# A second GEMM in two passes, with eight pairs of row blocks in the seven-product scheme

## The chip, the core and the metric

The kernel runs on one core of a Trainium2 chip. Its time is the device time of one execution in microseconds. The engines have short names throughout: PE (matmuls) with PEld (its weight loads), DVE (vector), ACT (scalar), POOL (GpSimd, which here only issues the accumulating transfers) and SP (which issues all other transfers).

## What is computed

The output is the sum of three terms over a sequence of S = 2048 rows with D = 1024 channels: the input itself, a gated long convolution, and a feed-forward network with F = 3584 hidden columns.

```python
xn = layernorm(q)                                   # rows of 1024
kv = short_causal_conv(k, shift_k, 4 taps) * v
y  = irfft(rfft(kv, 2S) * rfft(ssm_k, 2S))[:S] + kv * ssm_D
out = q + xn * y + silu(xn @ w1) @ w2               # w1: 1024 x 3584, w2: 3584 x 1024
```

Everything is f32. A matmul operand is split into two f16 parts, `hi` and `lo`, and a product takes three matmuls: hi.hi, hi.lo and lo.hi. The split is one ACT instruction (`hi`) and then one on DVE (`lo`), which needs ACT's result; `split` (L365) issues both.

## The kernel before

**Order of the work.** The kernel is a set of Python generators, each a stream of operations (`Op`) with an engine, an estimated duration, and what it reads and writes. `Order.run` (L165) keeps a clock of estimates and picks the stream whose next operation could start first, less a bias that is given to `add`. So the order on each engine is fixed when the program is built; on the chip each engine goes through its list in order and waits on semaphores. `L` issues a transfer on SP, `G` an accumulating one on POOL (the transfer engines add to what stands at the destination, in device memory or on chip), `T` a group of matmuls on PE. `Token` and `flag` tell a generator when it may go on. Buffers come from `Ring` (whole tiles) and `Halves` (tiles that are given out whole, `pair`, or by halves, `tile`): `wo` (six, operands of PE), `hfs` (three, f32 results), `hts` (two, split results on their way out), and eight `places` of one tile each, which hold the left operand blocks in the first GEMM and w2 in the second.

**First GEMM** (`units`, L1001, matmuls at L964 to L966): h = silu(xn @ w1). Rows go in two halves `sp`, columns in 14 pairs `i` of two blocks of 128. A pair of row blocks and a pair of column blocks make a 2 x 2 block product, done with seven products (`PRODUCTS`, L39) in place of eight; pairs 0 and 1 of the first half are done plainly. `evacuate` (L927) copies and sums the products, applies silu, and leaves four blocks: `up` and `low`, two each. Blocks of plain pairs are split and written to `hs` in device memory (`blocks`, L888). Blocks of the pairs in `PAIRS` (8, 9, 12, 13) go through `quad` (L845), which forms the seven left operands of the second GEMM (A11, A12, A22 and the sums S1 to S4), splits them, and writes them to `hsf`.

**Second GEMM** (`feed_forward`, L1050; matmuls at L1096 to L1098). A step is three matmuls of 128 x 128 weights and 512 columns. First the plain blocks: for each half `h` of the output columns and each of 16 row tiles, five chunks of four blocks, whose w2 lies in the places of `W2PLACE`; `result` (L1232) scales the sum and adds it to the output with `G`. Then `units2` (L1114): eight units of two row tiles by both column halves, seven products of four steps each. `evacuate2` (L1176) copies the shared partial sums between PSUM banks, sums two of the four results on DVE, and issues one transfer for each of four output tiles. `load_h` (L1240) loads the left operands in the order of use.

**w2** (`norms_w2`, L1283; `load_w2`, L1358). The raw rows come by SP into `wraw` or `hfs`; differences such as B22 - B12 are formed on DVE, with one place (`hold`) for sums that live on; `split` writes the factors into the places of `FPLACE`.

**Convolution** (`convolution`, L1394), in eight groups of 128 channels, interleaved with both GEMMs. For each group: `loads` and `load_v` fetch k, v and the filter; `gate` forms kv and its norms; `signal_parts` and `parts_of` split kv and the filter and transpose kv by a transfer; `stage1` multiplies by the DFT matrix; `transforms` runs an FFT of eight, the product of spectra and the inverse on DVE (`spec`, `tmp`); `result_parts`, `stage1_inv` and `gated` come back and add to the output (`yt`). The next group's `stage1` may write `spec` only where the last group has been read (`taken`). `copies` (L1256) puts x into the output before anything is added to it.

Of the kernel before, what the change touches and what calls it, by code (L numbers as in the profile page):

```python
# [20 lines left out]
P = 128  # L21
# [21 lines left out]
PAIRS = (8, 9, 12, 13)  # L43
# [3 lines left out]
W2PLACE = [(2, 7, 6, 3, 4), (0, 1, 5, 2, 7)]  # L47
FPLACE = (6, 3, 4, 0, 1, 5, 2, 7)
# [3 lines left out]
RAWS = {"B11": [(0, 0)], "B21": [(1, 0)], "B22": [(1, 1)], "T1": [(0, 1), (0, 0)], "T2": [(0, 0)],  # L52
        "T3": [(1, 1), (0, 1)], "T4": [(1, 0)]}
# [238 lines left out]
def h3_ffn_kernel(ctx, tc, x, kp, vs, fs, shift, dskip, w1, w2, cfwd, cinv, out):  # L292
# [82 lines left out]
    hs = [dram.tile([4, P, NF, 2, P], F16, name=f"hs{b}") for b in range(4)]  # L375
    ws = {i: {n: dram.tile([P, 2, KH, len(n) * P], F16, name=f"ws{i}_{n[0]}") for n in FACTORS} for i in range(2, NP)}
    xsp = {p[0]: dram.tile([P, 4, KH, 2, P], F16, name=f"xsp{p[0]}") for p in PRODUCTS.values()}
# [510 lines left out]
    def blocks(i, b, hf, tok, ready):  # L888
# [8 lines left out]
        for j in range(2):  # L897
            yield L(hs[b][:, :, 2 * i + j].rearrange("q p h s -> p q (h s)"),
                    ht[:, 4 * j:4 * j + 4].rearrange("p q h s -> p q (h s)"))
            ttok.set()  # L900
# [26 lines left out]
    def evacuate(i, b, one, c, made, seen):  # L927
# [5 lines left out]
        yield vs_r.ready  # L933
        u, ut = vs_r.tile([P, 4, P])
        yield made["P6"]
        yield a_act(u, two, AF.Copy)
# [4 lines left out]
        yield ws_r.ready  # L941
        d, dt = ws_r.tile([P, 4, P])
        yield made["P5"]
        yield a_act(d, two, AF.Copy)
        seen["P5"].set()
        low, done = yield from places_of(i, b + 1)
        yield v_tt(low[:, 1], c[0], d, ADD)
        dt.set()
# [4 lines left out]
        yield v_tt(low[:, 0], c[0], u, ADD)  # L953
        ut.set()
# [95 lines left out]
    def feed_forward():  # L1050
# [13 lines left out]
        for h in range(2):  # L1064
            for ts in TOGETHER[h]:
# [18 lines left out]
        flag["last part"].set()  # L1084
        yield from units2()


    TOGETHER = ([range(3)] + [(t,) for t in range(3, NT)],
                [(t,) for t in range(NT - 3)] + [range(NT - 3, NT)])

    def steps2(po, hx, wc, first, last, more=False, of=range(4), q=slice(0, W)):
        o = po[:, q]
        for n in of:
            def mm(n=n):
                kw = dict(skip_group_check=more)
                nc.tensor.matmul(o, hx[:, n, 0, :], wc[:, n, 0, q], start=first and n == 0, stop=False, **kw)  # L1096
                nc.tensor.matmul(o, hx[:, n, 0, :], wc[:, n, 1, q], start=False, stop=False, **kw)  # L1097
                nc.tensor.matmul(o, hx[:, n, 1, :], wc[:, n, 0, q], start=False, stop=last and n == 3, **kw)  # L1098
# [4 lines left out]
    def uses2():  # L1103

        yield 0, "P1"
        for u in range(len(tiles2)):
            for n in ("P7", "P6", "P2", "P5"):
                yield u, n
            if u + 1 < len(tiles2):
                yield u + 1, "P1"  # L1110
            yield u, "P3"
            yield u, "P4"

    def units2():  # L1114

        def product2(n, u, o, first=False, of=range(4), q=slice(0, W)):
            yield flag["h2", u, n]
            hx, htok = flag["h2", u, n].what
            yield flag["w2f", n]
            wc, wtok = w2f[n]  # L1120
            yield from steps2(o, hx, wc, first, True, not first, of, q)
            if 3 not in of or q.stop < W:
                return
            htok.set()
            if u == len(tiles2) - 1:
                wtok.set()

        yield ff.ready
        one = ff.tile([P, W])
        yield from product2("P1", 0, one[0], True)  # L1130
        for u in range(len(tiles2)):
            made, seen = defaultdict(Token), defaultdict(Token)
            last = u == len(tiles2) - 1
            yield ff.ready
            c = ff.tile([P, W])
            add(evacuate2(u, one, c, made, seen), EB)
            yield from product2("P7", u, c[0], True)
            yield seen["P1"]
            two = seen["bank"][0]
            yield from product2("P6", u, two)  # L1140
            made["P6"].set()
            if last:
                yield from product2("P2", u, one[0], of=(0, 1))
            else:
                yield from product2("P2", u, one[0])
                made["P2"].set()
            yield seen["P6"]
            yield from product2("P5", u, two)
            made["P5"].set()
            if last:  # L1150
                yield from product2("P2", u, one[0], of=(2, 3))
                made["P2"].set()
            else:
                yield ff.ready
                one = ff.tile([P, W])
                yield from product2("P1", u + 1, one[0], True)
            yield seen["P5"]
            yield from product2("P3", u, two)
            made["P3"].set()
            yield seen["P7"]  # L1160
            for q in columns(u):
                yield from product2("P4", u, c[0], q=q)
                made["P4", q.start].set()

    def columns(u):

        m = 2 if u == len(tiles2) - 1 else 1
        return [slice(a * W // m, (a + 1) * W // m) for a in range(m)]
# [7 lines left out]
    def evacuate2(u, one, c, made, seen):  # L1176
# [715 lines left out]
```

## Time and profile before

| | |
|---|---|
| median of 3 runs | 1251.4 us (1251.26 to 1251.9) |
| the profiled execution | 1250.78 us, span 1249.0 us |
| busy PE / PEld | 1227.0 us (98%) / 591.7 us (47%) |
| busy DVE / ACT / POOL | 1127.2 us (90%) / 749.5 us (60%) / 132.9 us (11%) |
| first GEMM's last matmuls, second's first | near 597 us |
| transfers | 292.9 MB: 266.9 MB by SP's queue (67.4% of the 16 transfer engines' span), 24.9 MB by POOL's (14.9%) |

A group's row reads: line, engine, operation, output<-inputs by the program's names, partitions x elements, xcount, then busy us and mean ns of one, then the idle time of the engine just before them and what ended it. Busy time of PE overstates its work, since matmuls overlap: their distance is what counts. L344, L347 and L355 are helpers that issue all sums, scaled sums and ACT instructions, so there the names of the tiles tell which step it is.

### The profile page before, as it was taken

The numbers are of one execution on the slowest core, as the hardware profiler recorded it, in microseconds if no ns is written. First come the engines' busy times: TensorE is split into PE (matmuls) and PEld (weight loads), VectorE is DVE, ScalarE is ACT, GpSimd is POOL, SyncE is SP. The second block draws the span as 40 slices with busy tenths as digits, with TensorE's granted clock in tenths as the row PEclk, the third lists the DMA queues.
The fourth block names the chain that finished last, engine by engine and source line by source line (L and its number), as shares of the span: only waits on it lengthen the run. The fifth ranks groups of instructions, "written<-read, shape, count | busy, mean of one in ns | idle before, by whom it ended". The sixth has DMA issues, their size and how long they took to land.

```text
span 1249.0 us, 17052 instructions
## 1 busy us (share of the span) xinstructions
PE 1227.0 (98%) x6017; PEld 591.7 (47%) x6017; DVE 1127.2 (90%) x1390; ACT 749.5 (60%) x1309; POOL 132.9 (11%) x141
## 2 busy tenths in 40 slices
PE   7899999999999999999999999999999999999998
PEld 6444544444444454445444544544454454445444
DVE  7999997889799979999899799889979979998992
ACT  6868897878767786757762632563273264526231
POOL 0000000000000030001110300310030030113114
PEclk8999999999999999999999999999999999999999
DMA  9358999889999898978998897689586587978766
GB/s 336 94 176 289 314 309 309 276 277 349 321 332 299 263 260 272 258 239 230 345 329 213 178 266 176 149 245 276 127 199 184 131 169 245 250 157 143 161 144 93
DMA packets 254293, 292.93 MB, mean 235 GB/s; under 512 B 48768, under 2 KB 167808, under 8 KB 252032
## 3 DMA queue, kind: packets, MB, share of 16 engines
q1 hardware_dynamic: 227472, 266.93, 67.4%
q0 software_dynamic: 26736, 24.92, 14.9%
q8 instruction: 47, 0.77, 0.2%
q14 instruction: 38, 0.31, 0.1%
HBM read 193.22 MB, written 98.57 MB: 234 GB/s over the span
## 4 chain that ended last, share of the span: by engine, by line
PE 69%; DVE 20%; issue 4%; DMA 4%; ACT 2%; POOL 0%; SPq 0%; DVEq 0%; POOLq 0%; ACTq 0%
PE ff L1096 10%; PE ff L1098 10%; PE ff L1097 10%; PE ff L966 10%; PE ff L964 10%; PE ff L965 10%; DVE spec L344 7%; DVE tmp L344 3%; DVE x L347 2%; PE ps L1563 2%; PE ps L1565 2%; PE ps L1564 2%; DVE spec L347 1%; DVE ht L347 1%; DMA out<-yt 1%
## 5 line engine op out<-in xcount | busy, mean ns | idle before, releaser
L1096 PE MATMUL ff<-x,wo 128*128 128x512 f16 x868 | 328.1, 378 | 1.0 <-DVE hf L347 0.6
L1098 PE MATMUL ff<-x,wo 128*128 128x512 f16 x868 | 328.1, 378 | 0.0
L1097 PE MATMUL ff<-x,wo 128*128 128x512 f16 x868 | 328.1, 378 | 0.0
L965 PE MATMUL ff<-x,wo 128*128 128x512 f16 (+1 forms) x808 | 303.9, 376 | 2.7 <-DVE x L347 2.7
L964 PE MATMUL ff<-x,wo 128*128 128x512 f16 (+1 forms) x808 | 303.9, 376 | 2.2 <-ACT wo L355 1.5
L966 PE MATMUL ff<-x,wo 128*128 128x512 f16 (+1 forms) x808 | 303.8, 376 | 1.7 <-DVE wo L347 0.9
L344 DVE TENSOR_TENSOR spec<-spec 128x1024 f32<-128x1024 f32 (+2 forms) x272 | 263.2, 1000 | 2.3
L1098 PEld LDWEIGHTS <-wo 128*128 128x128 f16 x868 | 84.9, 98 | 101.5
L1096 PEld LDWEIGHTS <-wo 128*128 128x128 f16 x868 | 84.9, 98 | 100.7
L1097 PEld LDWEIGHTS <-wo 128*128 128x128 f16 x868 | 84.9, 98 | 100.7 <-issue 1.4
L966 PEld LDWEIGHTS <-wo 128*128 128x128 f16 x808 | 79.4, 98 | 98.3 <-issue 3.3
L964 PEld LDWEIGHTS <-wo 128*128 128x128 f16 x808 | 79.4, 98 | 90.7 <-ACT wo L355 1.7
L965 PEld LDWEIGHTS <-wo 128*128 128x128 f16 x808 | 79.4, 98 | 88.5 <-issue 1.1
L341 POOL DMA_DIRECT2D out<-hf x59 | 52.2, 885 | 449.4 <-ACT hf L355 363.4
L355 ACT ACTIVATE hf<-ff,invc 128x512 f32<-128x512 f32 x60 | 40.9, 682 | 97.8 <-PE ff L1098 68.5
L341 POOL DMA_DIRECT2D out<-yt x56 | 63.1, 1327 | 333.1 <-DVE yt L347 189.6
L344 DVE TENSOR_TENSOR tmp<-spec 128x2048 f32<-128x2048 f32 (+1 forms) x48 | 92.6, 1934 | 0.9
L347 DVE SCALAR_TENSOR_TENSOR ht<-hf,wsc,ht 128x1024 f16<-128x1024 f32 (+1 forms) x56 | 67.3, 1204 | 12.5 <-ACT ht L355 12.4
L355 ACT ACTIVATE spec<-spec 128x1024 bf16<-128x1024 f32 x32 | 33.8, 1055 | 70.7 <-DVE spec L344 70.6
L347 DVE SCALAR_TENSOR_TENSOR wo<-raw,wsc,wo 128x512 f16<-128x512 f32 (+1 forms) x56 | 56.6, 1014 | 11.3 <-ACT wo L355 10.9
L355 ACT ACTIVATE spec<-ps 128x512 f32<-128x512 f32 x96 | 55.3, 590 | 16.6 <-PE ps L1565 14.9
L355 ACT ACTIVATE ht<-hf,wsc 128x1024 f16<-128x1024 f32 (+1 forms) x56 | 60.7, 1085 | 4.4 <-DVE hf L344 3.0
(173 smaller groups left out, 1753.6 us busy)
## 6 DMA issues: line engine op xcount, KB each, us to landing
wo<-hs SPq DMA_DIRECT2D x160, 256.0 KB, 3.7
hs<-ht SPq DMA_DIRECT2D x80, 256.0 KB, 4.6
wraw<-in_w SPq DMA_DIRECT2D x31, 512.0 KB, 5.3
out<-hf POOLq DMA_DIRECT2D x59, 256.0 KB, 4.3
raw<-in_w SPq DMA_DIRECT2D x28, 512.0 KB, 6.0
kin<-in_kp SPq DMA_DIRECT2D x16, 704.0 KB, 5.6
kf<-in_fs SPq DMA_DIRECT2D x8, 1024.0 KB, 5.3
hsfS<-ht SPq DMA_DIRECT2D x32, 256.0 KB, 4.5
```

The source lines that it names most:

```text
L341: return Op("POOL", 1.1, 4.8, lambda: nc.gpsimd.dma_start(o, i, accum_op=ADD), [i], [o], m, n)
L344: return V(lambda: nc.vector.tensor_tensor(o, a, b, op=op), o, [a, b], **k)
L347: return V(lambda: nc.vector.scalar_tensor_tensor(o, a, s, b, op0=op0, op1=op1), o, [a, b] + ([] if isinstance(s, float) else [s]), **k)
L355: nc.scalar.activation(o, i, func, scale=scale, **kw)
L964: nc.tensor.matmul(o, w[:, 0, k], xf[:, :, k, 0], start=first and k == 0, stop=False, **kw)
L965: nc.tensor.matmul(o, w[:, 0, k], xf[:, :, k, 1], start=False, stop=False, **kw)
L966: nc.tensor.matmul(o, w[:, 1, k], xf[:, :, k, 0], start=False, stop=last and k == KH - 1, **kw)
L1096: nc.tensor.matmul(o, hx[:, n, 0, :], wc[:, n, 0, q], start=first and n == 0, stop=False, **kw)
L1097: nc.tensor.matmul(o, hx[:, n, 0, :], wc[:, n, 1, q], start=False, stop=False, **kw)
L1098: nc.tensor.matmul(o, hx[:, n, 1, :], wc[:, n, 0, q], start=False, stop=last and n == 3, **kw)
L1563: nc.tensor.matmul(o, cf[:, 0], hi[i], start=i == 0, stop=False, **kw)
L1564: nc.tensor.matmul(o, cf[:, 0], lo[i], start=False, stop=False, **kw)
```

## The change

- `PAIRS` becomes eight of the fourteen pairs. 16 blocks of h are then multiplied in the seven-product scheme and 12 plainly (three chunks of four).
- The second GEMM runs in two passes. For column half 0 the plain part and then `pass_a` with the products P1, P6, P2, P7; for half 1 the plain part and then `pass_b` with P5, P3, P4. A product has eight steps, its factor lies in two places (`NR` = 4 blocks each), and its left operand is a whole `wo` tile of 512 KB.
- The four results of a unit are no longer put together on chip. Each intermediate sum is scaled by ACT (`taken`) and added to all output tiles that contain it by `G`: four transfers for a unit in `pass_a`, three in `pass_b` (at the last unit the last one is summed on DVE and written by SP, as before).
- The factors' differences are formed by transfers: ACT negates a raw tile, and `G` adds the other block of w2 to it (`less`, `difference2`). T2 is written to device memory (`t2s`) in the first pass and read for T4 in the second. Raw w2 is loaded in tiles of two rows.
- `evacuate` no longer takes two halves of `hfs` for copies; it copies into the result tile `low`, which it takes earlier.
- The convolution: v is loaded whole, from the `loads` stream, into a `kin` tile or a pair of `hl`; the squares of the filter go into the unused `acc` tile; in group 0 k's second half, v and the split kv lie in free parts of `spec`.

```diff
-PAIRS = (8, 9, 12, 13)
+PAIRS = (4,5,8,9,10,11,12,13)
+NR = NQ // 2
-W2PLACE = [(2, 7, 6, 3, 4), (0, 1, 5, 2, 7)]
-FPLACE = (6, 3, 4, 0, 1, 5, 2, 7)
+W2PLACE = [(2, 7, 6), (3, 0, 1)]
+FPLACE = {"P1": (3, 0), "P6": (1, 5), "P2": (4, 2), "P7": (7, 6), "P5": (5, 4), "P4": (2, 7), "P3": (6, 3)}
+PASSES = (("P1", "P6", "P2", "P7"), ("P5", "P3", "P4"))
...
-        flag["last part"].set()
-        yield from units2()
+            if h == 1:
+                flag["last part"].set()
+            yield from (pass_a, pass_b)[h]()
...
+    def taken(src, to, after):
+        yield lambda: hfs.ready() or flag["h end"]() and wo.ready()
+        o, otok = (wo if flag["h end"]() and wo.ready() else hfs).tile([P, W], uses=len(to))
+        yield a_act(o, src, AF.Copy, invc2[:, 0:1])
+        for t in after:
+            t.set()
+        yield flag["copied", 1]
+        for a in to:
+            yield G(a, o)
             otok.set()
...
+    def pass_a():
...
+        yield from first(0)
+        for u in range(n):
+            if u + 1 < n:
+                yield from first(u + 1)
+            yield seen["P1", u]
+            one, two = ones_[u], seen["bank", u]
+            yield from product2("P6", u, two[0])
+            add(taken(two[0], [at(u, 0, 1)], [seen["P6", u]]), EB)
+            yield from product2("P2", u, one[0])
+            add(taken(one[0], [at(u, 0, 0)], [one[1]]), EB)
+            yield seen["P6", u]
+            yield from product2("P7", u, two[0])
+            add(taken(two[0], [at(u, 1, 0), at(u, 1, 1)], [two[1]]), EB)
...
+    def pass_b():
...
+            yield seen["P5", u]
+            yield from product2("P3", u, fives[u][0])
+            add(taken(fives[u][0], [at(u, 0, 1)], [fives[u][1]]), EB)
...
+            for q in columns(u):
+                yield from product2("P4", u, four[0], True, q=q)
+                made[q.start].set()
+            if u < n - 1:
+                add(taken(four[0], [at(u, 1, 0)], [four[1]]), EB)
...
+    def less(t, other):
+        yield a_act(t, t, AF.Copy, -1.0)
+        yield G(t, other)
+
+    def difference2(name, of, k, t, tok):
+        yield from less(t, block2(of, k))
+        if name == "P6":
+            yield G(t, block2("B11", k))
+        split2(name, k, t, tok)
+        if name == "P6":
+            yield L(t2s[:, 2 * k:2 * k + 2], t)
+            tok.set()
+
+    def factors_a():
+        for k in range(NQ // 2):
+            yield from room2("P1", k)
+            b11, tok = yield from next_w2()
+            split2("P1", k, b11, tok)
+        for name, of in (("P6", "B22"), ("P2", None), ("P7", "B22")):
+            for k in range(NQ // 2):
+                yield from room2(name, k)
+                raw, tok = yield from next_w2()
+                if of is None:
+                    split2(name, k, raw, tok)
+                else:
+                    add(difference2(name, of, k, raw, tok), 0.05)
...
         def loads():
...
+                    if (g, b) == (0, 1):
+                        kin, tok = slots_of(13, 3)
...
-        def load_v():
...
+                    if g == 0:
+                        v, tok = slots_of(8 * b, 2)
...
+                    else:
+                        yield lambda: kin_r.ready() or hl_r.pairs()
...
+                    yield L(v[:, 0:T2], vs[g, b])
```

More of the change, by code (lines that the diff above doesn't have):

```diff
@@ L932, in evacuate @@
         seen["P1"].set()
[L933 to L934 removed]
+        low, done = yield from places_of(i, b + 1)
         yield made["P6"]
[L936 removed]
+        yield a_act(low[:, 0], two, AF.Copy)
         seen["P6"].set()
@@ L1114, in units2 @@
[L1114 to L1163, printed above, removed]
@@ L1195, in evacuate2, with first, end @@
+    def pass_b():
+        n = len(tiles2)
+        fives, seen = {}, defaultdict(Token)
+        def first(u):
+            yield ff.ready
+            fives[u] = ff.tile([P, W])
+            yield from product2("P5", u, fives[u][0], True)
+            add(taken(fives[u][0], [at(u, 1, 1)], [seen["P5", u]]), EB)
+        def end(u, four, made):
             yield flag["conv out"]
```

292 lines of the change are left out of this document (144 added, 148 removed).

## The prediction

> **What bounds the kernel now.** I read the page's busy shares first, then the busy times by stage, then the ends of the timeline, then who waits for whom.
>
> ```profile
> span 1249.0 us, 17052 instructions
> ## 1 busy us (share of the span) xinstructions
> PE 1227.0 (98%) x6017; PEld 591.7 (47%) x6017; DVE 1127.2 (90%) x1390; ACT 749.5 (60%) x1309; POOL 132.9 (11%) x141
> ```
>
> PE is busy for 98% of the span, so matmuls taken away should count. But DVE stands at 90%, and the stages show where its other 10% lies:
>
> ```profile
> 50.00:350.00 300.00, 297.80 (x1427) 140.30 (x1428) 267.25 (x381) 240.95 (x397) 1.71 (x2) 1.00 0.85 281
> 350.00:600.00 250.00, 248.11 (x1201) 116.96 (x1200) 231.92 (x269) 180.53 (x303) 17.19 (x16) 1.00 0.91 271
> 600.00:650.00 50.00, 50.00 (x235) 22.66 (x233) 49.86 (x49) 32.04 (x57) 4.86 (x5) 1.00 1.07 348
> 650.00:1200.00 550.00, 547.85 (x2663) 259.73 (x2662) 510.44 (x564) 246.57 (x467) 91.14 (x95) 1.00 0.78 192
> 1200.00:1249.00 49.00, 43.69 (x239) 23.00 (x236) 26.85 (x33) 12.57 (x20) 17.32 (x18) 0.99 0.67 108
> ```
>
> The columns are stage, length, then busy time (and count) of PE, PEld, DVE, ACT, POOL, then the granted clock (1.00, so nothing to gain there), the DMA share and GB/s. DVE idles 300 - 267.25 = 32.7 us between 50 and 350, and 18.1 + 0.1 + 39.6 = 57.8 us between 350 and 1200. What that idle time waited for, in 100 to 350 and then in 350 to 1220:
>
> ```profile
> DVE wo L347 <- ACT wo L355: 10.9, 14, 2.1
> DVE ht L347 <- ACT ht L355: 10.8, 10, 2.0
> ```
>
> ```profile
> DVE spec L344 <- ACT spec L355: 29.2, 12, 7.3
> DVE tmp L344 <- ACT spec L355: 9.2, 12, 2.8
> ```
>
> Early, DVE waits for the first half of a split (ACT writes `hi`, DVE then `lo`): more queued work fills such gaps. Later, 38.4 of the 57.8 us lie at the change from one group of the convolution to the next (spectrum copies by ACT): these belong to its dependent chain and stay. So the convolution is a second path nearly as long as PE's. Its last instructions on DVE and POOL:
>
> ```profile
> 1213.21 2.36 DVE L344 TENSOR_TENSOR spec<-spec 128x1024 f32<-128x1024 f32 x2
> 1215.48 1.28 DVE L347 SCALAR_TENSOR_TENSOR zl<-spec,csc,zh 128x1024 f16<-128x1024 f32 x1
> ...
> 1228.66 0.74 DVE L347 SCALAR_TENSOR_TENSOR wo<-ps,csc,ht 128x512 f32<-128x512 f32 x1
> ```
>
> ```profile
> 1230.67 2.20 POOL L341 DMA_DIRECT2D out<-wo x2 [0.25 <-DMA out<-wo]
> ```
>
> With 4.1 us to landing (row further below) its last output lands at 1230.67 + 2.20 + 4.1 = 1237.0. The span is 1249.0, so the convolution has 12.0 us in hand. This slack decides the forecast.
>
> **What leaves PE.** The second GEMM now takes 2 x 16 tiles x 5 chunks x 4 steps plain, and 8 units x 7 products x 4 steps: 864 steps of three matmuls. After the change it is 2 x 16 x 3 x 4 + 8 x 7 x 8 = 832. The 32 steps less are 96 matmuls of 512 columns. Their price is not the 378 ns of the group's row, which overlaps the next matmul, but the distance of starts:
>
> ```profile
> 1225.21 0.38 PE L1096 MATMUL ff<-x,wo 128*128 128x512 f16 x1
> ...
> 1240.53 0.38 PE L1098 MATMUL ff<-x,wo 128*128 128x512 f16 x1
> ```
>
> 71 steps lie between these two of 72 neighbours: 15.32 / 71 = 0.216 us. A step of three is 0.648 us, and the saving 96 x 0.216 = 20.7 us. The first GEMM keeps its matmuls. The last tile still splits its last product into two column halves, so the tail behind PE stays.
>
> **What DVE gets.** Prices by form, and two of ACT:
>
> ```profile
> L347 DVE SCALAR_TENSOR_TENSOR ht<-hf,wsc,ht 128x1024 f16<-128x1024 f32 x48 | 61.3, 1280 | 9.9 <-ACT ht L355 9.9
> ...
> L355 ACT ACTIVATE ht<-hf,wsc 128x1024 f16<-128x1024 f32 x48 | 55.0, 1146 | 4.2 <-DVE hf L344 3.0
> ...
> L355 ACT ACTIVATE hf<-ff,invc 128x512 f32<-128x512 f32 x60 | 40.9, 682 | 97.8 <-PE ff L1098 68.5 <-issue 17.8 <-DMA out<-hf 10.4
> ...
> L344 DVE TENSOR_TENSOR spec<-tmp 128x1024 f32<-128x1024 f32 x16 | 19.3, 1221 | 0.0
> ...
> L347 DVE SCALAR_TENSOR_TENSOR x<-x,tau,x 128x512 f16<-128x512 f32 x12 | 8.8, 747 | 0.0
> ...
> L344 DVE TENSOR_TENSOR hf<-hf 128x512 f32<-128x512 f32 x8 | 5.5, 687 | 0.1
> ```
>
> - In the first GEMM four more pairs go through `quad`, each for both halves `sp`: 8 quads. One costs 4 sums (4 x 0.69) and seven half blocks split (3 x 1.28 + 0.75) in place of four (2 x 1.28): 2.75 + 2.03 = 4.8 us, in all +38.2, half of it in each `sp`.
> - Plain weights of w2: 8 splits of 1024 less, -10.2. Factors: 56 splits of 512 for 28, +20.9. Factor differences leave DVE for POOL's transfers, 16 x 0.69 = -11.0. Sums at the end of each tile: 15 fewer of 0.75 and one sum of 0.69, -11.9. The gate multiplies 16 x 1024 in place of 32 x 512, 19.5 for 22.0, -2.5. Together -14.7.
>
> Net DVE: +23.5 us. The 12 units of `sp` 0 take 12 x 28 steps x 0.648 = 218 us from about 100 on, so their 19.1 us fall before 350, where 32.7 us are idle, 21.7 of them waits for ACT; I take them as hidden there (uncovered, they cost 19.1). The group-0 loads, which now go into free parts of `spec` and need no small ring, may start the first transform earlier; no row prices it, so between 0 and the 13.6 us of idle then left, nearest to 0 because loads are only one of the waits: -3. The 19.1 us of `sp` 1 and the -14.7 fall into the chained part, +4.4. Convolution end: 1237.0 + 4.4 - 3 = 1238.4.
>
> ACT gets 28 x 0.7 - 8 x 1.15 for splits, 16 negations of 1.15, 15 more evacuations of 0.68 and 8 x 1.9 for quads, about +54 us: near 65% of a span of 1230, no bound, though each wait of ACT for a transfer stands ahead of its PSUM evacuations.
>
> **What the transfers get.** 24 more accumulating transfers of 256 KB to `out` (4 + 3 a unit in place of 4, the last of all by SP now as then) and 20 of 512 KB into raw w2 tiles. Rows, from 1150 to 1200, then from the whole run:
>
> ```profile
> q0 software_dynamic: 1662, 2.92, 40.9%
> ...
> out<-hf POOLq DMA_DIRECT2D x12, 256.0 KB, 4.1
> ```
>
> ```profile
> L341 POOL DMA_DIRECT2D out<-hf x59 | 52.2, 885 | 449.4 <-ACT hf L355 363.4 <-DVE hf L347 48.3 <-ACT ps L355 12.6
> ```
>
> ```profile
> hf<-in_w SPq DMA_DIRECT2D x10, 512.0 KB, 6.2
> ```
>
> 40.9% of 50 us over 12 transfers is 1.70 us of all 16 engines per 256 KB. The addition is 24 x 1.70 + 20 x 3.40 = 109 us. From 600 to the end the share now sums to 53.5 + 429 + 32.8 = 515 us of 649; 624 would lie in about 628 us, a share of 1.0. In the row of 600 to 650 it was 1.07 at 348 GB/s and PE stayed at 50.00 of 50: loads run ahead in `wo`, six pairs, about 30 us of matmuls. I take PE's loss as 0, bounded above by the excess of the densest phase: in the first plain part (192 steps x 0.648 = 124 us) 12 of the 20 differences, 41 us, join a share of 0.78 to 1.07, 14 to 50 us over. The Trainium skill, page DMA: Bandwidth & Descriptors, section Specifications, gives about 27 GiB/s per engine, by which 256 KB would take an estimated 0.57 us and the addition 36 us; the measured 1.70 us speaks for more than one pass per byte and decides here.
>
> On POOL the 44 issues are 44 x 0.9 = 40 us on an engine busy 11%. Behind each waiting issue stand the outputs of tiles and of the convolution (`yt`), and for them wait `hf` buffers. The new chain at pass one: place 6 falls free only when the first plain part ends, and P7 needs its second half there 4.5 products x 8 steps x 0.648 = 23.3 us later. The chain is negation 1.15, issue 0.9, landing 4.1 to 6.2, two splits about 2.2: 8.4 to 10.5 us, and one more load of 6.2 and a second chain for the last tile, 23 to 27 at worst. Cost 0 to 4 us of PE; I take 1.
>
> **Sum**, against the profiled 1250.78 us (1.8 above its span; the median 1251.4 is 0.6 more). PE's path: 1250.8 - 20.7 + 1 = 1231.1. The convolution's: 1238.4 + 1.8 = 1240.2. The later one counts: 1240, with the 0.6 about 1241.
>
> **The rivals.**
> - *PE stays the bound.* If more than 13.5 us of DVE idle vanish, the convolution ends by 1229 and the full saving shows: 1231. For it: early waits that only lack work. Against it: 38 us of group changes. Chance 0.2.
> - *DVE becomes the bound and gives all back.* If nothing of `sp` 0 is hidden, and nothing comes from group 0, its end is 1237.0 + 23.5 = 1260.5, time 1263. It turns slower once more than 12.0 + 2.5 us of the 23.5 stay. For it: ACT at 241 of 300 early, so splits may wait as often as now. Between forecast and this end lies no change. Chance 0.15.
> - *Late factors or transfers hold PE.* Differences arriving 10 to 50 us late per pass, 1241 to 1280, likeliest 1255. For it: a share of 1.0 and waits at the head of ACT's and POOL's queues. Against it: the 1.07 row. Chance 0.15. The Trainium skill, SBUF — State Buffer, the "DVE blocks DMA" warning, has a POOL transfer take five times as long beside a DVE copy; here issues took 0.89 us with DVE busy 98%, so I give it nothing extra.
> - *The matmuls don't go*, and DVE's additions alone are left, 1255: the loop counts speak against it, 0.02.
>
> **How the numbers follow.** The forecast, 1236 to 1248, has 0.48. About 0.2% (2.5 us) is what a measurement of this kernel tells from no change. Faster: 0.48 + 0.2 + 0.02 of the third, 0.70. Same: 0.06, half each from the second and the third. Slower: 0.12 + 0.10 of these two and the last 0.02, 0.24. The range runs from PE's path, 1229, to 1259, leaving out the upper part of two rivals.
>
> **What would show it.** Right: 840 instructions in each matmul group of the second GEMM; DVE near 1150 us; its idle before 350 down to about 15; the last `yt` transfers landing within 5 us of the end. Wrong: PE waits of over 5 us in total for factors or `hx` loads; early DVE idle that stays at 33 us, or later idle over 58 us (then slower); either of them far below (then 1231).

## The result: 1293.85 us, 3.3% slower

The changed kernel takes 1293.85 us (median of 4 runs, 1291.57 to 1295.93) against 1251.65 for the kernel before beside it. The ratio is 1.0333, 95% interval 1.0318 to 1.0349. The forecast was 1241, its range 1229 to 1259.

The profiled execution of the changed kernel took 1291.57 us. The head of its page:

```profile
span 1289.8 us, 16919 instructions
## 1 busy us (share of the span) xinstructions
PE 1223.7 (95%) x5939; PEld 587.9 (46%) x5939; DVE 1149.2 (89%) x1410; ACT 790.5 (61%) x1344; POOL 178.9 (14%) x185
```

The amounts are those of the forecast: DVE was expected near 1150 us, POOL gets its 44 transfers (141 to 185 instructions). The matmuls went too. In the groups by line, each of the three matmul lines of the second GEMM now has 840 instructions:

```profile
L1094 PE MATMUL ff<-x,wo 128*128 128x512 f16 (+1 forms) x840 | 319.1, 380 | 10.2 <-ACT hf L358 9.7 <-DVE tmp L347 0.4
```

So the work is as planned, and it takes longer. The busy times by stage say where (stage, length, then PE, PEld, DVE, ACT, POOL, the granted clock, DMA share, GB/s):

```profile
50.00:350.00 300.00, 294.07 (x1394) 137.61 (x1395) 283.54 (x403) 241.99 (x392) 1.70 (x2) 0.99 0.84 280
350.00:600.00 250.00, 248.33 (x1200) 116.91 (x1199) 236.81 (x276) 181.07 (x290) 11.94 (x11) 1.00 0.96 286
600.00:650.00 50.00, 48.09 (x228) 22.18 (x227) 45.69 (x49) 31.61 (x54) 15.00 (x14) 1.00 1.12 324
650.00:800.00 150.00, 127.82 (x584) 58.22 (x583) 116.48 (x127) 74.88 (x142) 32.08 (x32) 0.93 1.10 268
800.00:950.00 150.00, 145.95 (x701) 68.16 (x700) 134.45 (x148) 69.02 (x128) 31.56 (x34) 1.00 0.87 202
950.00:1000.00 50.00, 41.47 (x201) 20.20 (x200) 32.93 (x39) 31.48 (x50) 21.16 (x20) 0.93 1.04 238
1000.00:1200.00 200.00, 196.78 (x960) 93.41 (x959) 184.17 (x199) 99.34 (x184) 40.35 (x42) 1.00 0.82 199
1200.00:1290.00 90.00, 80.64 (x425) 41.20 (x422) 73.67 (x76) 23.48 (x40) 24.41 (x25) 0.97 0.64 115
```

The same two stretches of the kernel before:

```profile
650.00:800.00 150.00, 149.97 (x731) 71.19 (x730) 141.47 (x156) 64.49 (x126) 18.48 (x20) 1.00 0.77 198
950.00:1000.00 50.00, 50.00 (x236) 22.67 (x234) 49.27 (x56) 14.71 (x35) 3.45 (x4) 1.00 0.57 144
```

From 650 to 800 PE falls from 150.0 busy us to 127.8 and from 731 matmuls to 584. There the transfer engines are full (share 1.10 at 268 GB/s), and even the granted clock falls to 0.93. These are the stretches where the factors' differences are formed. All five engines have idle time there; none of them is the bound.

**One measure is used below: PE's lost time.** For each two neighbouring matmuls of the timeline from 50 us on, it is the distance of their starts less the full pace (0.216 us for 512 columns, 0.108 for 256, 0.26 for f32 blocks), summed to PE's last matmul of the second GEMM. It comes from all PE rows of a trace, and contains stops and slow pace. Before it was 7.7 us (3.7 ahead of the second GEMM, 4.0 in it); after it is 64.7 (10.6 and 54.1). PE's last matmul ends at 1244.3 before and 1281.0 after. Less the lost time that is 1236.6 and 1216.3: **20.3 us of work did leave PE, against 20.7 forecast, and 57.0 us of standing came.** The span ends 8.7 us after PE's last matmul, 4.7 before; with these 4.0 the sum is -20.3 + 57.0 + 4.0 = 40.7 of the 40.8 us between the two profiled runs. What ends last in the changed kernel are the convolution's outputs on POOL; its last step on DVE ends at 1282.2, level with PE.

What PE waited for, longest in total first (us in total, times, longest):

```profile
PE ps L1602 <- ACT tmp L358: 10.5, 3, 5.8
PE ff L1094 <- ACT hf L358: 9.7, 3, 6.7
PE ps L457 <- ACT hl L358: 7.1, 1, 7.1
PE ps L1602 <- ACT spec L358: 6.5, 3, 3.5
PE ff L330 <- ACT hf L358: 5.3, 2, 3.6
```

Neither factors nor left operands stand in this list. PE waits for ACT: for PSUM banks that ACT should have copied out (`hf`), and for convolution steps (`tmp`, `spec`, `hl`) whose matmuls stand in the same list as those of the GEMM. And ACT, in the stretch from 594 to 986, waited first of all for buffers whose output has not landed; before, no wait for an output is among the seven longest there. The first row is of after, the second of before:

```profile
ACT hf L358 <- DMA out<-hf: 35.9, 11, 9.6
```

```profile
ACT spec L355 <- DVE spec L344: 52.3, 14, 7.6
```

One stop can be followed through from end to end. The timeline of the changed kernel, from SP, POOL, ACT, DVE and PE in turn (start, us, engine, line, output<-input, and idle time before it with its releaser):

```profile
648.96 1.21 POOL L344 DMA_DIRECT2D hf<-in_w  x1 [2.88 <-issue]
657.32 1.21 POOL L344 DMA_DIRECT2D hf<-in_w  x1 [1.36 <-DMA hf<-in_w]
...
646.43 0.39 SPq L335 DMA_DIRECT2D wo<-hs  x1
660.94 0.33 SPq L335 DMA_DIRECT2D t2s<-hf  x1
661.36 0.91 SPq L335 DMA_DIRECT2D wo<-hs  x2
...
653.93 0.69 ACT L358 ACTIVATE hf<-ff,invc 128x512 f32<-128x512 f32 x1 [9.59 <-DMA out<-hf]
660.95 1.34 ACT L358 ACTIVATE x<-hf,tau 128x512 f16<-128x512 f32 x2 [5.95 <-DMA hf<-in_w]
...
661.70 1.41 DVE L350 SCALAR_TENSOR_TENSOR x<-hf,tau,x 128x512 f16<-128x512 f32 x2 [10.13 <-ACT x L358]
673.02 1.22 DVE L347 TENSOR_TENSOR acc<-acc,hl 128x1024 f32<-128x1024 f32 x1
...
674.27 1.06 ACT L358 ACTIVATE hl<-acc 128x1024 f32<-128x1024 f32 x1 [2.20 <-DVE acc L347]
...
675.47 0.16 PE L457 MATMUL ps<-css,oneb 128*128 128x4 bf16 x1 [7.06 <-ACT hl L358]
675.50 0.59 PE L1094 MATMUL ff<-x,wo 128*128 128x512 f16 x1
675.88 0.63 PE L1095 MATMUL ff<-x,wo 128*128 128x512 f16 x1
```

POOL issues the second addition to the first raw tile (block B11) at 648.96; the first, issued at 628.77, had landed at 639.8. The second lands about 12 us later, near 660.9 (the chain of waits shows 11.96 us for it; a plain load of 512 KB of w2 took a median of 6.2 in the kernel before). SP's next instruction is the store of T2, `t2s<-hf`; it stands for 14 us, and two loads of `wo` stand behind it. ACT waits 9.59 us for a buffer of `hf` whose output is on its way, copies one bank, and then waits 5.95 us for the difference itself before it can split it. DVE's half of the split stands at the head of DVE's list, which waits 10.13 us. The work that piled up there reaches the convolution's gate only at 673.02; ACT squares it, and PE, whose next instruction is the small matmul for that norm, stands for 7.06 us. Then it goes on at 0.38 to 0.43 us a matmul where 0.216 is its pace, until 679.3. A late transfer has become a stop of PE by way of three in-order lists, 26 us after its issue. This shows one way from a landing to PE; what such waits for landings cost in all is for the runs below.

### The profile page after: what moved, and what is told of

Its sections match the earlier page's. It is cut to its first block, busy times and chain, and to the rows that moved or that the text cites. A ratio compares the mean times of both kernels' runs of the same rounds, so it can differ in the third digit from the quotient of the medians.

```text
span 1289.8 us, 16919 instructions
## 1 busy us (share of the span) xinstructions
PE 1223.7 (95%) x5939; PEld 587.9 (46%) x5939; DVE 1149.2 (89%) x1410; ACT 790.5 (61%) x1344; POOL 178.9 (14%) x185
## 4 chain that ended last, share of the span: by engine, by line
PE 55%; DMA 14%; issue 11%; DVE 11%; ACT 4%; POOL 4%; SPq 0%; POOLq 0%; DVEq 0%; ACTq 0%
PE ff L962 12%; PE ff L964 12%; PE ff L963 12%; PE ff L1094 5%; PE ff L1096 5%; PE ff L1095 5%; DMA out<-yt 3%; DVE spec L347 3%; POOL out L344 3%; DMA out<-hf 3%; DMA hf<-in_w 2%; DMA hl<-ht 2%; DMA wraw<-in_w 2%; DVE x L350 2%; DVE tmp L347 2%
## 5 line engine op out<-in xcount | busy, mean ns | idle before, releaser
L1094 PE MATMUL ff<-x,wo 128*128 128x512 f16 (+1 forms) x840 | 319.1, 380 | 10.2 <-ACT hf L358 9.7
L1095 PE MATMUL ff<-x,wo 128*128 128x512 f16 (+1 forms) x840 | 318.8, 380 | 0.0
L1096 PE MATMUL ff<-x,wo 128*128 128x512 f16 (+1 forms) x840 | 318.7, 379 | 0.0
L963 PE MATMUL ff<-x,wo 128*128 128x512 f16 (+1 forms) x808 | 304.6, 377 | 2.5 <-DVE x L350 2.5
L962 PE MATMUL ff<-x,wo 128*128 128x512 f16 (+1 forms) x808 | 304.6, 377 | 2.3 <-ACT wo L358 1.0
L964 PE MATMUL ff<-x,wo 128*128 128x512 f16 (+1 forms) x808 | 304.3, 377 | 1.7 <-DVE wo L350 0.9
L1095 PEld LDWEIGHTS <-wo 128*128 128x128 f16 x840 | 82.6, 98 | 107.0 <-issue 13.9
L1094 PEld LDWEIGHTS <-wo 128*128 128x128 f16 x840 | 82.6, 98 | 104.9 <-issue 10.4
L1096 PEld LDWEIGHTS <-wo 128*128 128x128 f16 x840 | 82.6, 98 | 99.2 <-issue 3.0
L344 POOL DMA_DIRECT2D out<-hf x82 | 76.1, 976 | 357.3 <-ACT hf L358 335.4
L964 PEld LDWEIGHTS <-wo 128*128 128x128 f16 x808 | 79.5, 98 | 98.6 <-issue 4.2
L962 PEld LDWEIGHTS <-wo 128*128 128x128 f16 x808 | 79.5, 98 | 91.2 <-ACT wo L358 1.4
L963 PEld LDWEIGHTS <-wo 128*128 128x128 f16 x808 | 79.5, 98 | 90.3 <-issue 3.1
L358 ACT ACTIVATE hf<-ff,invc 128x512 f32<-128x512 f32 x74 | 50.3, 684 | 87.6 <-PE ff L1096 42.5
L1602 PE MATMUL ps<-hl,cfw 128*128 128x512 f16 x120 | 46.8, 390 | 20.6 <-ACT tmp L358 10.5
L358 ACT ACTIVATE ht<-hf,wsc 128x1024 f16<-128x1024 f32 (+1 forms) x56 | 57.3, 1026 | 12.9 <-DVE hf L347 5.1
L350 DVE SCALAR_TENSOR_TENSOR ht<-hf,wsc,ht 128x1024 f16<-128x1024 f32 (+1 forms) x56 | 62.9, 1126 | 2.6 <-ACT ht L358 2.4
```

Of the source, the lines that this page charges most:

```text
L344: return Op("POOL", 1.1, 4.8, lambda: nc.gpsimd.dma_start(o, i, accum_op=ADD), [i], [o], m, n)
L350: return V(lambda: nc.vector.scalar_tensor_tensor(o, a, s, b, op0=op0, op1=op1), o, [a, b] + ([] if isinstance(s, float) else [s]), **k)
L358: nc.scalar.activation(o, i, func, scale=scale, **kw)
L962: nc.tensor.matmul(o, w[:, 0, k], xf[:, :, k, 0], start=first and k == 0, stop=False, **kw)
L963: nc.tensor.matmul(o, w[:, 0, k], xf[:, :, k, 1], start=False, stop=False, **kw)
L964: nc.tensor.matmul(o, w[:, 1, k], xf[:, :, k, 0], start=False, stop=last and k == KH - 1, **kw)
```

## The experiments

Times are medians; ratios are to the kernel before in runs on the same chip, with 95% intervals. Lost is PE's lost time in the profiled run; that of a4 leaves out 204 small matmuls on zeros, 30.4 us busy, that fill gaps there.

| label | time, us | ratio | lost, us |
|---|---|---|---|
| the change | 1293.85 | 1.0333 [1.0318, 1.0349] | 64.7 |
| a2_no_t2s | 1286.95 | 1.0269 [1.0245, 1.0292] | 63.1 |
| a8_scratch | 1286.5 | 1.0273 [1.0242, 1.0304] | 59.0 |
| a9_plain_scratch | 1263.62 | 1.0080 [1.0053, 1.0106] | 37.2 |
| a1_no_diff | 1255.67 | 1.0020 [1.0005, 1.0035] | 32.4 |
| a13_few_out | 1250.84 | 0.9992 [0.9976, 1.0009] | 25.0 |
| a10_no_quad_sums | 1249.89 | 0.9974 [0.9953, 0.9994] | 23.1 |
| a14_few_out_no_sums | 1246.04 | 0.9939 [0.9915, 0.9962] | 23.4 |
| a5_dve_diff | 1268.82 | 1.0132 [1.0107, 1.0158] | 28.5 |
| a4_order_real | 1300.91 | 1.0370 [1.0345, 1.0396] | 48.8 |
| a3_conv_old | 1328.73 | 1.0612 [1.0576, 1.0647] | 62.0 |
| a6_dve_conv_old | 1316.37 | 1.0501 [1.0482, 1.0521] | 28.9 |
| b1_conv_new | 1263.08 | 1.0085 [1.0057, 1.0114] | 17.0 |
| a11_quad_pool | 1301.24 | 1.0373 [1.0346, 1.0400] | 66.3 |
| a12_all_pool | 1336.98 | 1.0659 [1.0632, 1.0687] | 105.8 |
| c0_before_short | 1257.25 | 1.0041 [1.0025, 1.0058] | 11.1 |
| c1_no_diff_short | 1266.42 | 1.0108 [1.0089, 1.0127] | 43.9 |
| c2_after_short | 1291.9 | 1.0329 [1.0290, 1.0368] | 68.6 |

### Without the twenty transfers of the differences

```diff
-        yield from less(t, block2(of, k))
-        if name == "P6":
-            yield G(t, block2("B11", k))
         split2(name, k, t, tok)
```

> The changed kernel without the negations and the 20 accumulating transfers of 512 KB that form the factors' differences (so the factors are plain blocks of w2; everything else as changed). Theory 1, the differences are the cause (their landings come late and SP, ACT and DVE wait for them at the head of their lists): 1230 to 1250 us, PE waits in the first plain part and pass one gone. Theory 2, the 24 added transfers to the output and the busier transfer engines are the cause: at most half of the 42 us comes back, 1270 to 1285. Theory 3, the convolution's new loads are the cause: 1285 or more.

1255.67 us, ratio 1.0020: of the 42 us, 38 go with the differences. That is the way of theory 1 but 5.7 us above its range. What is left is about level with the kernel before and well above the 1231 of PE's path, so there is a second cause, smaller and paid back by the matmuls.

### The store of T2

```diff
-            yield L(t2s[:, 2 * k:2 * k + 2], t)
             tok.set()
...
-                    o = t2s[:, 2 * j:2 * j + 2]
+                    o = block2("B11", j)
```

> The changed kernel without the four stores of T2 on SP's queue; the second pass loads plain blocks in place of T2. Theory 1 in the form 'loads of PE's operands stand behind the stores on SP': the wait of 14 us near 647 goes, 1270 to 1282 us. Theory 2 (bandwidth): 4 MB of 317 less, under 5 us, 1289 or more. Theory 3: no change.

1286.95, ratio 1.0269, between the ranges of the theories: SP's list without the store is worth 7 to 8 us, and PE's lost time hardly moves (64.7 to 63.1). The 14 us wait on SP that the timeline shows is real, but mostly a symptom: without it the split of the same tile still waits for the landing.

### What in a difference costs: the wait, the accumulation, or the issue

In a8 the transfer adds to a strip of device memory that nobody reads, in a9 it copies there without adding.

```diff
-        yield G(t, other)
+        yield G(scr.pop(), other)      # a8
+        yield GP(scr.pop(), other)     # a9: nc.gpsimd.dma_start(o, i)
```

> The changed kernel with its negations and its 20 accumulating transfers of 512 KB, but each goes to a strip of device memory of its own that nobody reads, and the splits take the negated block at once (so the factors are not the differences). Theory 1a, what costs the 38 us is that the splits, the stores and the second accumulation wait for landings: about 1256 us as without the differences, up to 1265. Theory 1b, what costs it is the transfers' time on the 16 engines (68 us of it by the rows): 1280 to 1295.

> As the run into strips of memory that nobody reads, but the 20 transfers of 512 KB from POOL are plain copies, not accumulating ones (the factors are again not the differences). Theory 1b1, what costs is the transfer engines' time for reading, adding and writing: most of the 31 us over the run without differences go, 1256 to 1270 us. Theory 1b2, what costs is POOL's list and queue (the issues of outputs and buffers behind them) or the 16 negations on ACT: 1280 to 1290.

With a8 no split waits for an accumulation, and the time falls by 0.0060 of 1252, 7.5 us. With a9 it falls by another 0.0193, 24 us, and PE's lost time from 59.0 to 37.2. The issues on POOL, the blocks of w2 that are read and the list positions are the same in a8 and a9 but for the addition, so **the accumulation itself is the largest term**: not the dependence on it, and not POOL. From a9 to a1, where copies and negations go too, 0.0060 or 7.5 us are left. One thing is not tried apart: the change adds to tiles on chip, a8 to device memory. POOL's queue was equally busy in both. From 594 to 986 us, in the change, in a8 and in a9 (packets, MB, share of 16 engines):

```profile
q0 software_dynamic: 18395, 23.59, 39.2%
```

```profile
q0 software_dynamic: 18518, 23.78, 39.1%
```

```profile
q0 software_dynamic: 18145, 25.72, 34.2%
```

a9 moves more in the window (20 of these transfers for 16) and takes 4.9 points less of the engines, 19 us of all 16.

How this reaches PE is less clear. In the same window before and then after (issues: count, KB each, median us from issue to landing):

```profile
wo<-hs SPq DMA_DIRECT2D x134, 256.0 KB, 3.8
out<-hf POOLq DMA_DIRECT2D x26, 256.0 KB, 4.4
```

```profile
out<-hf POOLq DMA_DIRECT2D x46, 256.0 KB, 7.0
wo<-hs SPq DMA_DIRECT2D x48, 256.0 KB, 8.6
hf<-in_w POOLq DMA_DIRECT2D x11, 512.0 KB, 10.1
```

Transfers that the change did not touch take longer too: `wo<-hs` 8.6 us for 3.8, `out<-hf` 7.0 for 4.4. Most of that is not the addition's. From 650 to 800, with 21 to 23 loads of `wo<-hs` in each kernel, their median is 10.7 us in the change, 9.9 in a8, 8.6 in a9, 7.5 in a1 and 7.3 in a13; before it was 3.3. ACT copies through three `hf` buffers, and its waits from 594 to 986 until a landing set one free fall less evenly: 35.9 us in the change, 32.5 in a8, 22.8 in a9, 27.5 in a1, 16.8 in a13. So the waits for `hf` are there without the differences too, and how much of PE's loss runs through them is not shown. In a8 one stop of 5.9 us was for a load of left operands; the change has none.

How full the stage is shows better. The change and then a9, from 600 to 750 (columns as in the stages above):

```profile
600.00:750.00 150.00, 133.19 (x620) 61.30 (x619) 120.54 (x135) 78.11 (x144) 34.16 (x33) 0.95 1.14 291
```

```profile
600.00:750.00 150.00, 145.40 (x708) 68.98 (x707) 133.53 (x151) 93.79 (x167) 36.99 (x41) 1.00 1.08 322
```

The excess over a share of 1.0 is 21 us in the change, and PE is idle for 16.8; it is 15 in a8 for 9.3 idle, 12 in a9 for 4.6, and 7.5 in a1 and in a13 for 4.8 and 1.9. In all five the excess was an upper bound of PE's idle time.

### The plan's own price of a transfer

The order is fixed by estimates that count an accumulating transfer like a plain one. Here its bytes count 2.15 times.

```diff
-... [i], [o], m, n)
+... [i], [o], m, 2.15 * n)
```

> The changed kernel with the planner's estimate of an accumulating transfer's bytes times 2.15 (1.70 us measured per 256 KB where it reckons 0.79), so that only the order of the lists differs. Theory 4, the lists are ordered by estimates that put the readers of accumulated tiles too early: 1250 to 1275 us. Theories 1 and 2 with any order: within 10 us of 1294. Theory 3: no change.

1300.91, ratio 1.0370; the interval meets that of the change, so it is no faster, as theories 1 and 2 said. Where the plan foresees that PE will stand, it fills the gap with small matmuls on zeros. These groups, of after and then of a4:

```profile
L330 PE MATMUL ff<-one,zero 128*128 128x128 f32 x16 | 2.9, 314 | 5.3 <-ACT hf L358 5.3
```

```profile
L330 PE MATMUL ff<-one,zero 128*128 128x128 f32 x204 | 30.4, 311 | 13.4 <-ACT hf L358 12.2 <-DVE tmp L347 1.2
```

With 2.15 the plan foresees stops (204 fillers for 16), and the order that it finds doesn't avoid them. A higher price of the bytes alone does not mend it.

### Differences on DVE, and the convolution's loads

a5 forms the differences on DVE from 20 more plain loads and leaves nothing of the computation out. a3 and a6 put the old loads of the convolution back, into the change and into a5; b1 puts the new ones into the kernel before.

```diff
-        yield G(t, other)
+        other, done = yield from next_w2()
+        yield v_tt(t, other, t, op)
```

> The changed kernel with the differences formed on DVE from plain loads of the other blocks (20 loads of 512 KB on SP's queue and 20 sums of 1024 columns on DVE, 24 us of DVE). Theory 1a: the landings are waited for early, by loads that run ahead: 1256 to 1262 us if DVE's idle time hides the sums, 1270 to 1280 if they lengthen the convolution one for one. Theory 1b: 20 x 1.6 in place of 20 x 3.4 us on the transfer engines, about half back: 1270 to 1280 as well, but then with PE waits for transfers in the first plain part.

> The changed kernel with the convolution's loads and gate of before. Theory 5, the new loads cost here what they cost alone (9 to 10 us): 1280 to 1286 us. If the waits for the differences cover them: 1290 to 1296.

> Both of the last two edits: differences on DVE, the convolution's loads and gate of before. Theory 1a with theory 5: 10 us below the run with DVE's differences alone, 1246 to 1270, at best level with the kernel before. If the convolution's path alone sets the end, PE ends several us before the span.

> The kernel before with only the convolution's new loads and gate. Theory 3, these loads hold up the convolution: 1260 us or more. Otherwise 1245 to 1255.

a5 gains 25 us on the change but stays 1.3% slower than before. Its PE is done at 1241.7, and its convolution ends on DVE at 1259.0: here the convolution is the bound, with the 20.7 us that DVE got back (1169.9 busy for 1149.2). The old loads cost 35 us in the change and 46 in a5, far above every range given for a3 and a6 (at most 1296 and 1270). There the convolution's last step on DVE ends 43 us (a3) and 66 us (a6) after PE's last matmul: the changed kernel has no room for the old loads. In the kernel before, the new ones cost 0.0085, 11 us: the convolution's last step on DVE comes 4.9 us earlier (1229.4 to 1224.5), but PE loses 9.3 us more (7.7 to 17.0).

### DVE's sums: away, or on POOL

a10 is a1 without the 32 sums of the four added pairs; a11 is a5 with 64 sums of the quads on POOL, a12 with the differences there too.

```diff
-        yield v_tt(v, z, v, ADD)
+        yield p_tt(v, z, v, ADD)       # a11, a12: nc.gpsimd.tensor_tensor
```

> The run without differences, and also without the 32 DVE sums of the four added pairs (22 us of DVE in the first GEMM left out, so their left operands are not the sums). Theory 6, DVE's work on the convolution's path sets the end once the differences' transfers are gone: 1234 to 1246 us. If PE's waits set it: 1250 to 1257.

> The run with DVE's differences, and all 64 sums of the quads on POOL in place of DVE (44 us of DVE less, about 75 us of POOL more, nearly all in the first GEMM where POOL has nothing to do). Theory 6: the convolution ends 35 to 44 us earlier and PE's path takes over, 1238 to 1250 us, level with or below the kernel before. Against it: POOL's sums take so long that the split operands of the second GEMM or the buffers behind them come late, 1260 or more.

> As the last, and the 20 sums of the differences on POOL as well (24 us of DVE less, about 46 us of POOL more, in the second GEMM where POOL issues the output transfers). Theory 6: 1232 to 1245 us. If the sums hold up the output transfers behind them on POOL: 1250 to 1270, with waits of ACT for the buffers of outputs.

Taking 22 us of DVE away (a10) gives 0.0046, 6 us: DVE's busy time is not the sum that sets the end. The idle time between 50 and 350 us goes back up, from 17.9 in a1 to 30.2. POOL is no refuge. Its sum in a11:

```profile
L353 POOL TENSOR_TENSOR hf<-hf 128x512 f32<-128x512 f32 x16 | 31.0, 1941 | 431.4 <-DVE ht L356 413.5 <-DVE pow L500 17.9
```

1.94 us against DVE's 0.69, and the first GEMM has no slack for it: PE loses 40.3 us ahead of the second GEMM. a12 came 67 us above the upper end of its range. (The Trainium skill, page GPSIMD Engine Reference, section Elementwise — side-by-side cycle accounting, has a ratio of 1.96 for 2048 elements; here it is 2.8 for 512.)

### The rest: output transfers, and whether the convolution is it

a13 is a1 with as many output transfers as before the change; a14 is a13 without a10's sums.

```diff
-            add(taken(two[0], [at(u, 0, 1)], [seen["P6", u]]), EB)
+            add(taken(two[0], [None], [seen["P6", u]]), EB)
```

> The kernel without difference transfers and negations (a1, 1255.7), and 24 of its 56 output transfers fewer: of what passes a and b add to the output, P6's and P5's results and the second destination of P7's are left out (copies by ACT stay). POOL's accumulating transfers to the output are then as many as before the change. Theory T (the 24 added output accumulations, 24 x 1.70 = 41 us of all 16 transfer engines, still hold PE and the buffers): 8 to 15 us less, 1241 to 1248, and PE's lost time in the second GEMM falls from 21 us to under 10. Rival D (DVE's added work sets the end of the convolution, whatever the transfers do): within 4 us of a1, 1252 to 1256, with the end of the convolution on DVE still near 1250.

> As a13, and without the 32 DVE sums of the added quads (22 us of DVE; the seven left operands of four pairs are then not the sums). Theory T with D (both add up): 6 us less than a13, as a10 stood to a1, so 1236 to 1242. Theory P (with transfers and DVE both back at the load of before, only the 20.7 us of matmuls taken away are left, and PE's path shows): 1231 to 1236, PE's lost time in the second GEMM under 6 us. Rival R (a third cause, such as the convolution's new loads, the order on PE, or the early splits that wait for ACT, holds it): 1246 to 1252, no better than a10.

a13's ratio, 0.9992, is below a1's but the intervals meet; its median is 4.8 us lower, between what the two theories said, and nearer to the one that gives the outputs little. Neither theory's second sign came: PE's lost time in the second GEMM stays over 10 us (theory T), and the convolution's last step on DVE ends at 1236.5, not near 1250 (rival D). a14 reaches 1246.04, still 15 above PE's path, at the edge of what rival R said: with transfers and sums both back, a third cause is left.

The next three leave out ten sums and four scaled sums of the forward FFT on DVE in each group, in the kernel before, in a1 and in the change.

```diff
-            yield v_tt(C(0), C(2), C(3), ADD)
...
-                yield v_stt(flat[0], flat[1], r, flat[2], MUL, ADD)
             tok.set()
```

> The kernel before, with the convolution shortened on DVE: the 10 sums and 4 scaled sums that follow the first butterflies of the forward FFT of eight are left out in all eight groups, some 14 x 1.22 x 8 = 137 us of DVE. It takes the convolution off the path that sets the end, and is the measure for the next two. PE's path alone: 1244 to 1252 (PE lost only 7 us before).

> The same shortening in the changed kernel without difference transfers and negations (a1). Theory C (the rest of a1's loss, 15 to 25 us, is stops of PE on convolution steps that DVE brings later): the saving of 96 matmuls shows whole, 20.7 us less than the shortened kernel before, within 4 us. Rival T (transfers and loads hold PE on their own): 5 to 15 us less than the shortened kernel before, and PE still loses over 12 us.

> The same shortening in the changed kernel itself, with its 20 accumulating differences. Theory T2 (the differences hold PE directly, by late factors and by ACT behind late buffers): 20 to 35 us slower than the last kernel, and slower than the shortened kernel before by 5 to 15 us. Rival C2 (they cost because they delay the convolution's DVE chain, and PE waits for that): at most 10 us slower than the last kernel, and faster than the shortened kernel before by 10 us or more.

The convolution's last step on DVE, in c0, in c1 and in c2:

```profile
1090.05 0.74 DVE L347 SCALAR_TENSOR_TENSOR yt<-ps,csc,xg 128x512 f32<-128x512 f32 x1
```

```profile
1136.24 0.75 DVE L350 SCALAR_TENSOR_TENSOR yt<-ps,csc,xg 128x512 f32<-128x512 f32 x1 [1.14 <-DMA out<-yt]
```

```profile
1166.20 0.75 DVE L350 SCALAR_TENSOR_TENSOR yt<-ps,csc,ht 128x512 f32<-128x512 f32 x1 [4.42 <-DMA out<-yt]
```

The convolution now ends 158, 125 and 120 us ahead of PE, and no kernel gains from it: c0 is 5 us slower than before (1.0041, above its range), c2 level with the change (1.0329 against 1.0333), and c1 is slower than a1 by 0.0088. **So a convolution that ends earlier speeds up neither kernel.** In the change its outputs are the last 4 us; in c2 they are not, and PE itself ends 5.7 us later. (The order of the lists changes with the sums left out, so these runs test the end and not the price of a step.) c2 is 25 us slower than c1, as T2 said, and 36 slower than c0, beyond its 5 to 15: the differences hold PE without help from the convolution's end. But the theory that a1's rest is PE waiting for a late convolution falls, and its rival as well: c1 is 9 us slower than c0 where 5 to 21 less were expected, with 43.9 us lost. In c1 PE waits 8.7 us for PSUM banks and 10.2 for steps of the convolution. A reading that no run tests: each group's steps are a chain of ACT, DVE and PE however short the whole is, and the plan now puts more of them into the dense stretch.

## Why the prediction was wrong

- **The matmuls, −20.7: right.** 840 instructions a line, and 20.3 us between the two kernels' PE ends less lost time. In the ten variants with the new scheme, its loads and its plan's prices and no sums on POOL, PE's end less lost time lies between 1213 and 1219 (1236.6 before, 1237.7 in c0).
- **The failed step: "I take PE's loss as 0", and 0 to 4 for the chain at pass one.** PE's lost time rose by 57.0 us. The price of the transfers was near: 109 us of all 16 engines were forecast for the 44, and POOL's queue went from 14.9% of 1249.0 us to 22.0% of 1289.8, 98 us more. That this time would be covered was wrong: a8 against a9 shows the addition alone worth 24 us of run time. The upper bound, 14 to 50 us over in the first plain part, was worked out from it, and was then set aside for one row, 600 to 650 with a share of 1.07 and PE at 50.00 of 50. That row shows that PE survives a full share for 50 us while loads run ahead. It does not show what happens when results wait as well: in the changed kernel the first such 50 us, at 1.12, cost PE 1.9 us, and the next 150, at 1.10, cost 22.2, inside the bound that had been set aside.
- **Why the cover failed.** The prediction named the six pairs of `wo` that run ahead; they held in the changed kernel (no load of left operands is among PE's longest waits). What did not hold was the other side, ACT's list, where waits for `hf` buffers and for landed differences stand. The text said that each wait of ACT for a transfer stands ahead of its PSUM evacuations, and gave it no time. The stop shown above is one that came that way; how much of the 57.0 us did is open, as the waits for `hf` in a1 show.
- **The path.** The forecast took the convolution's end, 1240.2, for the later of two paths, and moved it by DVE's amounts alone, 1.4 us. The amounts came (1149.2 us; idle 50 to 350 down to 16.5 where about 15 was expected), the end did not: the last step on DVE ends 52.8 us later than before (1282.2 for 1229.4), together with PE. Late transfers hold both paths through the same lists. And c2 shows that a convolution ending 120 us ahead of PE makes the change no faster.
- **The later idle time "belongs to its dependent chain and stays".** From 350 to 1200 it went from 57.8 to 99.5 us. The group changes in it took less (29.4 us for 38.4); 36.4 us of it are one wait that was not among the longest before, DVE's half of a factor's split behind ACT's:

```profile
DVE x L350 <- ACT x L358: 36.4, 14, 10.1
```

- **Group 0's loads, −3.** On the convolution's end the sign was right (4.9 earlier in b1). The step forgot PE: the loads cost 11 us in b1 where nothing else changed.
- **The rivals.** "Late factors or transfers hold PE" (0.15) was the case, and its price, 1241 to 1280, still too low. The point that spoke against it, the 1.07 row, was the weak one. (For "PE stays the bound" the text asks for 13.5 us of idle time to vanish; by its own sum, 1240.2 - 1231.1, 9.1 beyond what it had counted would do. No chance hangs on that.)
- **How the 57.0 us divide**, by PE's lost time along the runs: 5.7 waits for landings of differences, and the destination in device memory (change to a8), 21.8 their accumulating (a8 to a9), 4.8 copies and negations (a9 to a1), 7.4 the added outputs (a1 to a13), 1.6 the quads' sums (a13 to a14), 15.7 the rest (a14 to before). b1 has 9.3 on its own for the convolution's loads, which would be the larger part of the rest if it adds up in the changed kernel (not shown); that could not be tried there, since the old loads do not fit (a3, a6). About 6 us stay open. The shares also depend on the order of the steps: taken away from a1, the quads' sums are worth 9.3 us of PE's time (a10), from a13 1.6. Single profiled runs stand behind each of these, so differences of one or two us say nothing.

No version that computes everything beats the kernel before. The nearest, a1, a10, a13 and a14, leave the differences out.

## What to carry to other kernels

A transfer that accumulates is not a free sum: price it by the share of the transfer engines that its rows show, and add it to the share of the stage in which it falls. Where that goes over 1.0, take the excess as an upper bound of PE's idle time and put a part of it into the sum: over 150 us a quarter to four fifths of it came true in the five kernels above, though single stretches of 50 us lost nothing (before at 1.07, a1 at 1.11). A step that is moved from a busy engine to transfers comes back as waits at the heads of in-order lists, and PE can pay where its list holds the matmuls of a second computation that is a chain of several engines. Before a path is called the later one, test it: one run with that path shortened shows whether it bounds anything.

## What the runs showed of the hardware

- After a stop of some us PE can run at half pace for a while. The timeline of after has five stops of 3.8 to 7.4 us (distance of starts) that are each followed by 7 to 13 matmuls at 0.43 us in place of 0.216, and one of 2.8 close behind another that is too; one of 3.0 is not, nor are those of up to 2.5. In all 60 matmuls are slow so, 12.4 us of the 64.7; before, one is. The page shows it as a granted clock of 0.93 from 650 to 800 and from 950 to 1000. The Trainium skill, page TensorE: Matmul & The Clock Gate, section HAM oscillation, describes idle gaps of over some 3.4 us that put the clock to half. The trace of after agrees: PE was idle for 3.5 to 7.1 us in those five. Elsewhere the border is not sharp: 2.2 us of idle time in b1 were followed by seven slow matmuls, 3.2 us in a8 by none.
- The addition in a transfer of 512 KB, to device memory, cost 1.2 us of run time for each of 20 (24 us, a8 against a9), without anyone reading the result. From 650 to 800 us POOL's queue moved 10.1 MB in both, at 39.4% of the engines in a8 and 31.8% in a9: an estimated 1.6 us of all 16 engines for each of some seven.
